# Later tiles' decayed keys and normed output: turned by VectorE blocks and a pass through DRAM in place of TensorE

## The chip, the cores and the metric

One core of a Trainium2 chip runs the whole program. The metric is the device time of one execution in microseconds (us); lower is better. The engines are named as in the profile: PE is TensorE (PEld its weight load), DVE is VectorE, ACT is ScalarE, POOL is GpSimd, SP is SyncE, which here issues nearly all DMAs.

## The reference, cut to what matters

Three stages follow each other. The first is gated linear attention over 4 sequences of 768 tokens with 8 heads of 48; the second a gated feed-forward layer on the normed output; the third a mixture of 8 experts, one per token.

```python
for t in range(S):
    state = alpha[:, :, t, :, None] * state + np.einsum('bhd,bhe->bhde', k[:, :, t], v[:, :, t])
    y[:, :, t] = np.einsum('bhd,bhde->bhe', q[:, :, t], state)
...
xn = x / rms * rms_g
g = xn @ w_gate
silu = g * (1.0 / (1.0 + np.exp(-g)))
val = xn @ w_val
return (silu * val @ w_out).astype(np.float32)
...
h = np.maximum(x[mask] @ w1[e], 0.0)
ye = h @ w2[e]
out[mask] = gate_w[mask, None] * eom[mask, e, None] * ye
```

## The kernel before, in words

The 3072 tokens are 24 tiles of 128 (t = 0 to 23). Tiles 0 to 17 go round over three sequences, so tile t is chunk t // 3 of sequence t % 3; tiles 18 to 23 are the fourth sequence in order. Chunk 5 of a sequence (tiles 15, 16, 17 and 23) is final and leaves no state behind.

**Attention of a tile.** Ahead of it comes the prework (`prework`, L365): alpha, k and q arrive by DMA, in `blk_a`, `blk_k`, `blk_q` from tile 7 on (`PET`, L239 to L260, twelve DMAs a tile), DVE turns them by 32x32 blocks (L386) so that the head dimension lies on partitions and tokens along the row, two scans on DVE (L315, L325) form the decays `Z` and `aT`, and two products (L407) the decayed keys `kT` and queries `qT`. Then `stages` (L411) has five stages:

- `score`: 8 matmuls `ps_s` (L426); DVE masks them into `P0`, `P1` (L436).
- `ktr`: 4 transposes on PE of `kT` into `ps_k` (L446), which ACT copies to `kn` (L448). Final tiles have none.
- `outp`: matmuls `ps_y` (L460, L464); ACT and POOL make the normed rows `xn` (L470 to L473).
- `state`: 8 matmuls `ps_st` (L485) from `kn` and `v`, added to the state by DVE (L492).
- `xtr`: 3 transposes on PE of `xn` into `ps_x` (L506). ACT scales them by `gT` (L512) and writes the high half `xh` (L513), DVE the low half `xl` (L514).

From tile 6 on `outp` and `state` share a place (`four`, L848).

**Feed-forward.** Three tiles are one group of 384 columns, whose `xh` and `xl` it needs. A group has 12 units; each is nine matmuls `ps_g`, nine `ps_v` (both at L608) and nine `ps_o` of the unit before (L642). ACT makes `tt` from `ps_g` (L600), DVE multiplies it with `ps_v` (L619), ACT writes `hh` (L622), DVE `hl` (L628). `ps_g` and `ps_v` have one PSUM bank each, so `tt` of a unit must be done with `ps_v` when the next unit's `ps_v` starts, and `hh` and `hl` when the next unit's `ps_o` starts.

**Order.** From the third group on (loop at L1091) one stage of attention is due every 2.4 slots, a slot being the nine matmuls of one kind, and `LEADG` says by how many slots the stages run ahead. PE keeps the order in which the matmuls were written (`seq`); on DVE, ACT and SP a scheduler orders the instructions when the program is built, and each engine then runs its list in order, as SP does with the DMAs: one that waits holds up those behind it. The eight experts follow from some 560 us on.

Of the kernel before, what the change touches and what calls it, by code (L numbers as in the profile page):

```python
# [40 lines left out]
    'TS': 3,  # L41
    'RA': 7,
    'RB': 9,
    'LEADG': 6,
    'NAT': 5,
    'XO': 2,
    'MT': 6,
    'STRICT': 4,
    'PET': 7,
    'NO': 'arkq',  # L50
}


# [2 lines left out]
def gla_glu_moe_kernel(  # L56
# [118 lines left out]
    def f(x):  # L175
        return x.bitcast(F32)
# [27 lines left out]

    vt = {}
    pre = {}
    xT = {}
    SEATS = CFG['SEATS']
    spread = [True]
    strict = [False]  # L210
# [93 lines left out]
    def flat(x):  # L304
        return x.rearrange("p a b -> p (a b)")
# [59 lines left out]
    def prework(t):  # L365
        if t < NAT:
            w = prework_nat(t)
            for x in CFG['NO']:
                yield w[x]
            return  # L370
        aT = att.tile([P, NP, P], F32, tag="aT", name="aT", bufs=CFG["ZBUF"])
        Z = att.tile([P, NP, P], F32, tag="A", name="Z", bufs=CFG["ABUF"])
        qT = att.tile([P, NP, P], F32, tag="qT", name="qT", bufs=2)
        kT = att.tile([P, NP, P], F32, tag="kT", name="kT", bufs=2)

        def tr(dst, nm):
            if t < PET:
                ps = bank([P, NP, P], "ps_n")
                src = rowt[nm].rearrange("p (a h) d -> p a (h d)", h=2)
                for p in range(NP):  # L380
                    nc.tensor.transpose(ps[:, p, :], src[:, p, :], ident)
                ins = nc.scalar.activation(dst, ps, AF.Copy)
                if t + 1 < PET:
                    load_tile(t + 1, nm)
                return ins
            return nc.vector.transpose(out=dst.rearrange("a p (c j) -> a p j c", j=TW),  # L386
                                in_=blk[nm].rearrange("a p (j d) -> a p j d", d=D)[:, :, :, 0:32])
        def tr_qk():
            tr(kT, "k")
            tr(qT, "q")  # L390
            if PET <= t + 1 < NTILE:
                load_tile(t + 1)
        def tra():
            now[0] = t
            ins = tr(aT, 'a')
            if t >= PET:
                pace(f'sc{t}', ins)
        yield tra
        yield tr_qk
        def sc():  # L400
            now[0] = t
            nc.gpsimd.memset(Z[:, NP - 1, P - 1:P], 1.0)
            pre[t] = (after_scan(Z, aT), qT, kT)
        yield sc
        yield lambda: upto_scan(aT, Z, aT)
        def mul(o, i):
            pace('km%d' % t, nc.vector.tensor_tensor(out=o, in0=o, in1=i, op=ALU.mult))  # L407
        yield lambda: mul(kT, Z)
        yield lambda: mul(qT, aT)

    def stages(t):  # L411
        b, c = place_of[t]
        first, final = c == 0, c == NCH - 1
        en, qT, kT = pre[t]
        Sc = state_of[b % BS]
        S_ = wide[0]
        rs = [slice(64 * hh, 64 * hh + D) for hh in range(2)]
        g, ti = divmod(t, GT)
        Pt = {}

        def score():
            ps = [bank([P, NP, P], "ps_s") for _ in range(2)]
            for p in range(NP):
                for hh in range(2):
                    r = slice(64 * hh, 64 * hh + D)
                    seq(nc.tensor.matmul(ps[hh][:, p, :], lhsT=kT[r, p, :], rhs=qT[r, p, :], start=True, stop=True))  # L426

            def post():
                if not first:
                    nc.vector.tensor_tensor(out=Sc, in0=Sc, in1=en.to_broadcast([P, NP, D]), op=ALU.mult)  # L430
                    for hh in range(2):
                        nc.scalar.activation(S_[rs[hh], :, hh * D:hh * D + D], Sc[rs[hh]], AF.Copy)
                mb = mask.to_broadcast([P, NP, P])
                for hh in range(2):
                    Ph = seat_of(t, f"P{hh}", [P, NP, P])
                    pace(f'Ph{t}', nc.vector.tensor_tensor(out=Ph, in0=ps[hh], in1=mb, op=ALU.mult))  # L436
                    Pt[hh] = Ph
            return post
        yield score

        def ktr():
            if final:
                return None
            ps = bank([P, NP, P], "ps_k")
            for p in range(NP):
                seq(nc.tensor.transpose(ps[:, p, :], kT[:, p, :], ident))  # L446
            kn = seat_of(t, "kn", [P, H, 64])
            nc.scalar.activation(kn, ps.rearrange("p a (h d) -> p (a h) d", h=2), AF.Copy)  # L448
            Pt["kn"] = kn
            return None  # L450
        yield ktr

        halves = (slice(0, 64), slice(64, P))

        def outp():
            ps = bank([P, DM], "ps_y")
            if not first:
                for p in range(NP):
                    for u in halves:
                        seq(nc.tensor.matmul(ps[u, p * 2 * D:p * 2 * D + 2 * D], lhsT=qT[:, p, u], rhs=S_[:, p, :],  # L460
                                         start=(p == 0), stop=False, skip_group_check=True))
            for h in (0, 2, 4, 6, 1, 3, 5, 7):
                for u in halves:
                    seq(nc.tensor.matmul(ps[u, h * D:h * D + D], lhsT=Pt[h % 2][:, h // 2, u], rhs=vt[t][:, h, :],  # L464
                                     start=first, stop=True, skip_group_check=True))

            def post():
                xn = seat_of(t, "xn", [P, DM])
                ss = att.tile([P, 1], F32, tag="ss", name="ss", bufs=2)
                pace(f'xs{t}', nc.scalar.activation(xn, ps, AF.Square, accum_out=ss))  # L470
                nc.gpsimd.tensor_scalar(out=ss, in0=ss, scalar1=1.0 / DM, scalar2=1e-6, op0=ALU.mult, op1=ALU.add)  # L471
                pace(f'ss{t}', nc.gpsimd.tensor_tensor(out=ss, in0=ss, in1=mhalf, op=ALU.pow))
                pace(f'xa{t}', nc.scalar.activation(xn, ps, AF.Copy, scale=ss[:, 0:1]))  # L473
                Pt["xn"] = xn
            return post
        yield outp

        def state():
            if final:
                return None  # L480
            kn = Pt["kn"]
            ps = bank([P, NP, D], "ps_st")
            for p in range(NP):
                for hh in range(2):
                    seq(nc.tensor.matmul(ps[64 * hh:64 * hh + 64, p, :], lhsT=kn[:, 2 * p + hh, :],  # L485
                                     rhs=vt[t][:, 2 * p + hh, :], start=True, stop=True))

            def post():
                if first:
                    nc.scalar.activation(Sc, ps, AF.Copy)  # L490
                else:
                    nc.vector.tensor_tensor(out=Sc, in0=ps, in1=Sc, op=ALU.add)  # L492
            return post
        yield state

        def xtr():
            if t and t + 2 < NTILE:
                load_v(t + 2)
            if ti == 0:
                xT[g] = (act.tile([P, KD, G], F32R, tag="xh", name="xh"),  # L500
                         act.tile([P, KD, G], F32R, tag="xl", name="xl"))
            xh, xl = xT[g]
            xn = Pt["xn"]
            ps = bank([P, KD, P], "ps_x")
            for kc in range(KD):
                seq(nc.tensor.transpose(ps[:, kc, :], xn[:, kc * P:kc * P + P], ident))  # L506
            sl = slice(ti * P, ti * P + P)

            def post():
                xf = xn.rearrange("p (a b) -> p a b", a=KD)  # L510
                for kc in range(KD):
                    pace(f'xg{t}', nc.scalar.activation(xf[:, kc, :], ps[:, kc, :], AF.Copy, scale=gT[:, kc:kc + 1]))  # L512
                pace(f'xh{t}', nc.scalar.activation(xh[:, :, sl], xf, AF.Copy))  # L513
                pace(f'xl{t}', nc.vector.tensor_tensor(out=xl[:, :, sl], in0=xf, in1=f(xh[:, :, sl]), op=ALU.subtract))  # L514
            return post
        yield xtr


    late = []

# [341 lines left out]
            return None  # L862
        return s_, k_, yd_, no_, x_

    att_stream = (st for t in range(GT, NTILE) for st in (four if t >= CFG['MT'] else stages)(t))
    nprep = GT + 1
    AHEAD = CFG['AHEAD']
    done = 0
# [222 lines left out]
    for g in range(2, NG):  # L1091
# [15 lines left out]
        for n in range(3 * KF):  # L1107
            post = slot(g + 2, n)
            if post:
                post()  # L1110
            if done < (NTILE - GT) * NST and ((g - 1) * 3 * KF + n + 1 + CFG['LEADG']) * GT >= (done + 1 - GT * NST) * 3 * KF / NST:
                post = stage()
                if post:
                    post()
# [274 lines left out]
```

## Time and profile before

| | |
|---|---|
| median of 3 runs | 851.7 us (851.08 to 854.45) |
| profiled execution, its own time | 854.62 us |
| its span, first to last instruction | 852.8 us |
| PE busy | 836.4 us (98%) |
| DVE busy | 493.9 us (58%) |
| ACT busy | 324.0 us (38%) |
| mean granted TensorE clock | 0.993 of full speed |

"Busy" is the time in which an engine runs at least one instruction. PE's matmuls overlap, so their cost is read from the distances of their starts, not from their durations. A releaser in square brackets names what ended an engine's idle time.

### The profile page before, as it was taken

The numbers are of one execution on the slowest core, as the hardware profiler recorded it, in microseconds if no ns is written. First come the engines' busy times: TensorE is split into PE (matmuls) and PEld (weight loads), VectorE is DVE, ScalarE is ACT, GpSimd is POOL, SyncE is SP. The second block draws the span as 40 slices with busy tenths as digits, with TensorE's granted clock in tenths as the row PEclk, the third lists the DMA queues.
The fourth block names the chain that finished last, engine by engine and source line by source line (L and its number), as shares of the span: only waits on it lengthen the run. The fifth ranks groups of instructions, "written<-read, shape, count | busy, mean of one in ns | idle before, by whom it ended". The sixth has DMA issues, their size and how long they took to land.

```text
span 852.8 us, 15908 instructions
## 1 busy us (share of the span) xinstructions
PE 836.4 (98%) x6196; PEld 802.5 (94%) x6196; DVE 493.9 (58%) x1111; ACT 324.0 (38%) x705; POOL 147.4 (17%) x204
## 2 busy tenths in 40 slices
PE   7999999999999999999999999999999999999996
PEld 6899999999999999999999999999998999999996
DVE  6899989496855656765666552243444342443341
ACT  1655544334233333332432332333235342454441
POOL 2001001001200100010010010013033242343351
PEclk8999999999999999999999999999999999999999
DMA  9955573872411322232232000042055164266421
GB/s 193 181 155 155 166 176 85 224 180 71 114 45 41 82 57 65 49 84 62 61 89 61 10 29 1 2 124 71 8 198 191 56 218 132 75 204 203 148 69 36
DMA packets 120269, 88.97 MB, mean 104 GB/s; under 512 B 55291, under 2 KB 115324, under 8 KB 120192
## 3 DMA queue, kind: packets, MB, share of 16 engines
q1 hardware_dynamic: 115728, 78.46, 35.2%
q0 software_dynamic: 4464, 9.48, 3.2%
q8 instruction: 49, 0.80, 0.4%
q14 instruction: 28, 0.23, 0.1%
HBM read 72.11 MB, written 16.07 MB: 103 GB/s over the span
## 4 chain that ended last, share of the span: by engine, by line
PE 80%; DMA 6%; DVE 5%; issue 4%; ACT 2%; POOL 1%; SPq 1%; POOLq 0%; DVEq 0%; ACTq 0%
PE ps_o L642 18%; PE ps_v L608 17%; PE ps_g L608 17%; PE ps_b L1071 8%; PE ps_h L608 7%; PE ps_s L426 3%; DMA st<-in_moe_w_dram 3%; PE ps_y L464 3%; PE ps_y L460 2%; DMA out_dram<-ob,ix 1%; DMA er<-bucket 1%; PE ps_x L506 1%; PE ps_k L446 1%; PE ps_st L485 1%; DMA blk_q<-in_q_dram 1%
## 5 line engine op out<-in xcount | busy, mean ns | idle before, releaser
L619 DVE TENSOR_TENSOR tt<-tt,ps_v 128x384 f32<-128x384 f32 x96 | 52.9, 551 | 123.2 <-PE ps_v L608 111.9
L622 ACT ACTIVATE hh<-tt 128x384 fp32r<-128x384 f32 x96 | 50.3, 524 | 132.0 <-DVE tt L619 124.7
L600 ACT ACTIVATE tt<-ps_g 128x384 f32<-128x384 f32 x96 | 47.1, 490 | 121.3 <-PE ps_g L608 116.2
L628 DVE TENSOR_TENSOR hl<-tt,hh 128x384 fp32r<-128x384 f32 x96 | 54.4, 566 | 27.4 <-ACT hh L622 26.7
L1056 DVE SCALAR_TENSOR_TENSOR h<-ps_h,h 128x256 fp32r<-128x256 f32 (+6 forms) x72 | 38.0, 531 | 54.2 <-ACT h L1055 53.8
L608 PE MATMUL ps_g<-xh,wgh 128*128 128x384 f32 x192 | 67.9, 354 | 0.0
L608 PE MATMUL ps_v<-xh,wvh 128*128 128x384 f32 x192 | 65.7, 342 | 1.4 <-DVE tt L619 1.4
L1071 PE MATMUL ps_b<-w2a,h 128*128 128x384 f32 (+2 forms) x336 | 66.6, 339 | 0.5 <-ACT h L1055 0.5
L642 PE MATMUL ps_o<-woh,hh 128*128 128x400 f32 x192 | 66.6, 355 | 0.0
L642 PE MATMUL ps_o<-wol,hh 128*128 128x400 f32 x192 | 66.4, 346 | 0.0
L1071 PE MATMUL ps_b<-w2b,h 128*114 128x384 f32 (+3 forms) x336 | 65.2, 338 | 0.4 <-ACT h L1055 0.2
L608 PE MATMUL ps_g<-xh,wgl 128*128 128x384 f32 x192 | 65.0, 338 | 0.1
L608 PE MATMUL ps_v<-xh,wvl 128*128 128x384 f32 x192 | 64.9, 338 | 0.0
L608 PE MATMUL ps_g<-xl,wgh 128*128 128x384 f32 x192 | 64.8, 338 | 0.0
L608 PE MATMUL ps_v<-xl,wvh 128*128 128x384 f32 x192 | 64.7, 337 | 0.0
L642 PE MATMUL ps_o<-woh,hl 128*128 128x400 f32 x192 | 63.4, 344 | 0.0
L1071 PEld LDWEIGHTS ps_b<-w2b,h 128*114 128x114 f32 (+3 forms) x336 | 57.4, 175 | 2.6 <-ACT h L1055 0.6
L1071 PEld LDWEIGHTS ps_b<-w2a,h 128*128 128x128 f32 (+2 forms) x336 | 57.7, 181 | 1.6 <-ACT h L1055 1.0
L608 PE MATMUL ps_h<-x,w1b 128*128 128x456 f32 (+3 forms) x288 | 58.6, 344 | 0.1
L1055 ACT ACTIVATE h<-ps_h 128x256 fp32r<-128x256 f32 (+6 forms) x72 | 33.3, 467 | 62.1 <-PE ps_h L608 57.3
L471 POOL TENSOR_SCALAR ss<-ss 128x1 f32<-128x1 f32 x24 | 8.2, 341 | 273.6 <-ACT xn L470 268.7
L608 PE MATMUL ps_h<-x,w1a 128*128 128x256 f32 (+3 forms) x288 | 53.6, 328 | 0.0
(284 smaller groups left out, 1966.6 us busy)
## 6 DMA issues: line engine op xcount, KB each, us to landing
st<-in_moe_w_dram SPq DMA_DIRECT2D x64, 384.0 KB
bucket<-zero SPq DMA_DIRECT2D x8, 772.0 KB
stg<-in_moe_w_gate_dram SPq DMA_DIRECT2D x12, 384.0 KB
stg<-in_moe_w_val_dram SPq DMA_DIRECT2D x12, 384.0 KB
stg<-in_moe_w_out_dram SPq DMA_DIRECT2D x12, 384.0 KB
v<-in_v_dram SPq DMA_DIRECT2D x23, 192.0 KB
blk_a<-in_alpha_dram SPq DMA_DIRECT2D x34, 96.0 KB
blk_k<-in_k_dram SPq DMA_DIRECT2D x34, 96.0 KB
```

Of the source, the lines that this page charges most:

```text
L426: seq(nc.tensor.matmul(ps[hh][:, p, :], lhsT=kT[r, p, :], rhs=qT[r, p, :], start=True, stop=True))
L460: seq(nc.tensor.matmul(ps[u, p * 2 * D:p * 2 * D + 2 * D], lhsT=qT[:, p, u], rhs=S_[:, p, :], start=(p == 0), stop=False, skip_group_check ...
L464: seq(nc.tensor.matmul(ps[u, h * D:h * D + D], lhsT=Pt[h % 2][:, h // 2, u], rhs=vt[t][:, h, :], start=first, stop=True, skip_group_check= ...
L600: nc.scalar.activation(tt, ps, AF.Silu)
L608: seq(nc.tensor.matmul(ps, lhsT=a_[:, kc, :], rhs=b_[:, kc, :], start=(n == 0), stop=(n == 3 * KD - 1)))
L619: nc.vector.tensor_tensor(out=tt, in0=tt, in1=ps, op=ALU.mult)
L622: nc.scalar.activation(hh, tt, AF.Copy)
L628: nc.vector.tensor_tensor(out=hl, in0=tt, in1=f(hh), op=ALU.subtract)
L642: seq(nc.tensor.matmul(obank[s][i], lhsT=a_[:, sl], rhs=weight(b_, j), start=(j == j0 and n == 0), stop=(j == j1 - 1 and n == 2)))
L1055: nc.scalar.activation(hh[:, 0, :], ps, AF.Relu)
L1056: nc.vector.scalar_tensor_tensor(out=hh[:, 1, :], in0=ps, scalar=0.0, in1=f(hh[:, 0, :]), op0=ALU.max, op1=ALU.subtract)
L1071: ins = nc.tensor.matmul(ob2[u][i][0:r], lhsT=hh[:, a_, sl], rhs=we[p][b_][:, j, :], start=(j == 0 and m == 0), stop=(j == KF2 - 1 and m = ...
```

## The change

From tile 9 on (`DT`) no tile is turned by PE, but for tile 9's keys.

- Keys: `turn_k(t + 1)` in the fourth stage of tile t. DVE turns `kT` by 32x32 blocks into `Z`, which is free by then; four DMAs write it to a DRAM buffer in runs of 32 floats (128 bytes, 512 runs each), so placed that the blocks come to lie where the full transpose wants them; one DMA reads the buffer back as `kn`. Tiles 10 to 14 and 18 to 22: ten times.
- Rows: `turn_x` in the fifth stage. DVE turns `xn` into the space of `P0`, four DMAs of 384 runs of 128 bytes write it to DRAM, one reads it back into `xn`. `put_x`, in the second stage of the next tile, does the scaling, `xh` and `xl`, from SBUF. Tiles 9 to 23: fifteen times.
- `LEADG` goes from 6 to 11 slots, and two stages are added at the end for the last tile's `put_x`.
- Tile 7's turns of `blk_k` and `blk_q`, the first from the block buffers, keep the order of the source on DVE.

```diff
-    'LEADG': 6,
+    'LEADG': 11,
+    'DT': 9,
...
-            return nc.vector.transpose(out=dst.rearrange("a p (c j) -> a p j c", j=TW),
+            ins = nc.vector.transpose(out=dst.rearrange("a p (c j) -> a p j c", j=TW),
                                 in_=blk[nm].rearrange("a p (j d) -> a p j d", d=D)[:, :, :, 0:32])
+            if t == PET and nm != "a":
+                tc.keep_in_program_order(ins)
+            return ins
...
-            kn = Pt["kn"]
+            kn = Pt["kn"] if "kn" in Pt else kq.pop(t)
...
+        def turn_x():
+            if t + 2 < NTILE:
+                load_v(t + 2)
+            xn, xb = Pt["xn"], flat(Pt[0])[:, 0:DM]
+            nc.vector.transpose(out=xb.rearrange("p (a k i) -> p k a i", a=TW, k=KD),
+                                in_=xn.rearrange("p (k d a) -> p k a d", a=TW, k=KD))
+            mid = dram.tile([P, KD * P], F32, tag="mid_x", name="mid_x", bufs=2)
+            dst = mid.rearrange("(d a) (k c i) -> c d (a k) i", a=TW, k=KD, c=TW)
+            for c in range(TW):
+                nc.sync.dma_start(dst[c], xb[32 * c:32 * c + 32].rearrange("d (n i) -> d n i", i=32))
+            nc.sync.dma_start(xn, mid)
+
+        def put_x():
+            group()
+            xh, xl = xT[g]
+            xf = Pt["xn"].rearrange("p (a b) -> p a b", a=KD)
+            sl = slice(ti * P, ti * P + P)
+            for kc in range(KD):
+                nc.scalar.activation(xf[:, kc, :], xf[:, kc, :], AF.Copy, scale=gT[:, kc:kc + 1])
+            nc.scalar.activation(xh[:, :, sl], xf, AF.Copy)
+            nc.vector.tensor_tensor(out=xl[:, :, sl], in0=xf, in1=f(xh[:, :, sl]), op=ALU.subtract)
+        moves[t] = (turn_x, put_x)
...
+    def turn_k(t):
+        Z, kT = spare[t], pre[t][2]
+        nc.vector.transpose(out=flat(Z).rearrange("a (c p d) -> a p c d", c=TW, p=NP),
+                            in_=kT.rearrange("a p (j c) -> a p c j", c=TW))
+        mid = dram.tile([P, H * 64], F32, tag="mid_k", name="mid_k", bufs=2)
+        dst = mid.rearrange("(j c) (p a d) -> a j (c p) d", c=TW, p=NP, a=TW)
+        for a in range(TW):
+            nc.sync.dma_start(dst[a], flat(Z)[32 * a:32 * a + 32].rearrange("j (n d) -> j n d", d=32))
+        kn = att.tile([P, H, 64], F32, tag="kn", name="kn")
+        nc.sync.dma_start(flat(kn), mid)
+        kq[t] = kn
...
+    def moved(t):
+        s_, k_, y_, d_, _ = stages(t)
+        def second():
+            if t == DT:
+                k_()
+            return laid.pop() if laid else None
...
+        def keys_():
+            while prep:
+                prep_step()
+            if t + 1 < NTILE and place_of[t + 1][1] < NCH - 1:
+                turn_k(t + 1)
+        def rows_():
+            moves[t][0]()
+            laid.append(moves[t][1])
+        return s_, second, yd_, keys_, rows_
```

How the built order moves is shown at three places. In the changed kernel the lines have other numbers: L386 is L389, L315 is L318, L325 is L328, L619 is L666, L622 is L669, L628 is L675, L600 is L647; the block turns of keys and rows are L556 and L512, their writes L561 and L517, their reads L563 and L518, the scaling of the read rows L526.

DVE at tile 7, in the second group, before; `F` and `Fo` are weights being unpacked:

```order
L534 SCALAR_TENSOR_TENSOR Fo<-stg,Fo 128x384
L386 STREAM_TRANSPOSE qT<-blk_q 128x4x4x32
L386 STREAM_TRANSPOSE kT<-blk_k 128x4x4x32
L531 SCALAR_TENSOR_TENSOR F<-stg,F 128x384
L619 TENSOR_TENSOR tt<-tt,ps_v 128x384
```

And now, from the same `Fo` on, and then from the row where the turns stand:

```order
L581 SCALAR_TENSOR_TENSOR Fo<-stg,Fo 128x384
L578 SCALAR_TENSOR_TENSOR F<-stg,F 128x384
L666 TENSOR_TENSOR tt<-tt,ps_v 128x384
L581 SCALAR_TENSOR_TENSOR F<-stg,F 128x384
L675 TENSOR_TENSOR hl<-tt,hh 128x384
```

```order
L666 TENSOR_TENSOR tt<-tt,ps_v 128x384
L389 STREAM_TRANSPOSE aT<-blk_a 128x4x4x32
L389 STREAM_TRANSPOSE kT<-blk_k 128x4x4x32
L389 STREAM_TRANSPOSE qT<-blk_q 128x4x4x32
L581 SCALAR_TENSOR_TENSOR F<-stg,F 128x384
L578 SCALAR_TENSOR_TENSOR Fo<-stg,Fo 128x384
```

The two turns stood ahead of the product `tt` of a unit; they now stand behind the `tt` of the second unit after it.

DVE at tile 20, before (`state` is the running state, `en` and `begin` small helpers of the scans):

```order
L386 STREAM_TRANSPOSE qT_5676<-blk_q_1470 128x4x4x32
L628 TENSOR_TENSOR hl_5537<-tt_5522,hh_5536 128x384
L492 TENSOR_TENSOR state0_122<-ps_st_5564,state0_122 128x192
L407 TENSOR_TENSOR qT_5426<-qT_5426,aT_5424 128x512
L430 TENSOR_TENSOR state0_122<-state0_122,en_5494 128x192
L386 STREAM_TRANSPOSE aT_5674<-blk_a_1467 128x4x4x32
L312 COPY en_5744<-aT_5674 128x4
L313 MEMSET aT_5674 128x4
L315 SCALAR_TENSOR_TENSOR Z_5675<-aT_5674,begin_127 128x511
L318 TENSOR_TENSOR en_5744<-en_5744,Z_5675 128x4
L324 RECIPROCAL begin_127<-Z_5675 128x4
L325 SCALAR_TENSOR_TENSOR aT_5674<-aT_5674,begin_127 128x512
```

And now:

```order
L675 TENSOR_TENSOR hl_5505<-tt_5489,hh_5504 128x384
L556 STREAM_TRANSPOSE Z_5408<-kT_5410 128x4x4x32
L389 STREAM_TRANSPOSE qT_5663<-blk_q_1470 128x4x4x32
L499 TENSOR_TENSOR state0_122<-ps_st_5543,state0_122 128x192
L414 TENSOR_TENSOR qT_5409<-qT_5409,aT_5407 128x512
L437 TENSOR_TENSOR state0_122<-state0_122,en_5473 128x192
L389 STREAM_TRANSPOSE aT_5661<-blk_a_1467 128x4x4x32
L512 STREAM_TRANSPOSE P0_5424<-xn_5552 128x3x4x32
L315 COPY en_5727<-aT_5661 128x4
L316 MEMSET aT_5661 128x4
L318 SCALAR_TENSOR_TENSOR Z_5662<-aT_5661,begin_127 128x511
L666 TENSOR_TENSOR tt_5570<-tt_5570,ps_v_5572 128x384
```

Two block turns have come in, and the first scan (L318) now writes a `Z` out of which the four writes of the keys are still reading, ahead of the unit's `tt`. SP's list for the same tile, now:

```order
L561 DMA mid_k<-Z 512x1x32 x4
L365 DMA v<-in_v_dram 128x8x48
L263 DMA blk_q<-in_q_dram 32x4x192
L263 DMA blk_q<-in_q_dram 32x4x160
L563 DMA kn<-mid_k 128x512
L263 DMA blk_a<-in_alpha_dram 32x4x192
L517 DMA mid_x<-P_5424 384x1x32 x4
L263 DMA blk_a<-in_alpha_dram 32x4x160
L263 DMA blk_a<-in_alpha_dram 32x4x192
L518 DMA xn<-mid_x 128x384
```

The ten DMAs of the two turns stand among the loads of the next tile's blocks, and each read back waits on SP for its four writes.

ACT at tile 20, before, from the normed rows (L473) on:

```order
L473 ACTIVATE xn<-ps_y,ss 128x384
L432 ACTIVATE wide_125<-state_122 48x4x48 x2
L600 ACTIVATE tt<-ps_g 128x384
L622 ACTIVATE hh<-tt 128x384
L512 ACTIVATE xn<-ps_x,gT 128x128 x3
L513 ACTIVATE xh<-xn 128x3x128
L600 ACTIVATE tt<-ps_g 128x384
```

And now (`xn` scaled at L526 from what the DMA brought back):

```order
L480 ACTIVATE xn<-ps_y,ss 128x384
L439 ACTIVATE wide_125<-state_122 48x4x48 x2
L647 ACTIVATE tt<-ps_g 128x384
L669 ACTIVATE hh<-tt 128x384
L647 ACTIVATE tt<-ps_g 128x384
L526 ACTIVATE xn<-xn,gT 128x128 x3
L527 ACTIVATE xh<-xn 128x3x128
L669 ACTIVATE hh<-tt 128x384
L647 ACTIVATE tt<-ps_g 128x384
```

The scaling stood one unit behind the normed rows and waited for PE; it now stands behind the second unit's `tt`, mostly ahead of its `hh`, and waits for a DMA.

## Rows read from the trace of the kernel before

**Rows 1.** The page's first part: busy time, share and instructions of each engine.
```profile
PE 836.4 (98%) x6196; PEld 802.5 (94%) x6196; DVE 493.9 (58%) x1111; ACT 324.0 (38%) x705; POOL 147.4 (17%) x204
```
**Rows 2.** Busy time by stretch: PE, PEld, DVE, ACT, POOL, clock, DMA share, GB/s.
```profile
115.00:170.00 55.00, 53.55 (x430) 51.09 (x429) 41.84 (x85) 22.14 (x54) 3.01 (x10) 1.00 0.57 153
230.00:260.00 30.00, 30.00 (x234) 29.19 (x233) 19.12 (x37) 10.21 (x25) 1.59 (x5) 1.00 0.30 71
400.00:490.00 90.00, 90.00 (x749) 86.81 (x748) 55.02 (x125) 30.83 (x74) 7.45 (x14) 1.00 0.21 52
```
**Rows 3.** Timeline of PE around one tile's key transposes: start, duration, instruction.
```profile
407.09 0.34 PE L608 MATMUL ps_v<-xh,wvle 128*128 128x384 f32 x1
...
407.89 0.34 PE L642 MATMUL ps_o<-wole,hh 128*128 128x400 f32 x1
```
**Rows 4.** Timeline of PE at tile 19, from the unit ahead of its output on.
```profile
435.49 0.34 PE L608 MATMUL ps_v<-xh,wvl 128*128 128x384 f32 x1
...
438.24 0.34 PE L642 MATMUL ps_o<-wol,hh 128*128 128x400 f32 x1
...
439.70 0.33 PE L608 MATMUL ps_g<-xh,wgh 128*128 128x384 f32 x1
...
444.28 0.34 PE L642 MATMUL ps_o<-woh,hl 128*128 128x400 f32 x1
444.46 0.49 PE L506 MATMUL ps_x<-ident,xn 128*128 128x128 f32 x3
...
444.97 0.34 PE L608 MATMUL ps_g<-xl,wgh 128*128 128x384 f32 x1
```
**Rows 5.** Timelines of DVE and of PE at tile 7.
```profile
116.41 1.11 DVE L386 STREAM_TRANSPOSE qT<-blk_q 128x512 f32<-128x512 f32 x1 [2.74 <-DMA blk_q<-in_q_dram]
...
119.33 0.44 PE L608 MATMUL ps_v<-xh,wvh 128*128 128x384 f32 x1 [1.45 <-DVE tt L619]
```
**Rows 6.** Groups on DVE, 230 to 545 us: busy, mean ns, idle before.
```profile
L325 DVE TENSOR_TENSOR_SCAN aT<-aT,begin 128x512 f32<-128x512 f32 x12 | 14.6, 1220 | 0.2
...
L386 DVE STREAM_TRANSPOSE kT<-blk_k 128x512 f32<-128x512 f32 x11 | 12.1, 1099 | 0.0
...
L407 DVE TENSOR_TENSOR kT<-kT,Z 128x512 f32<-128x512 f32 x12 | 8.0, 668 | 0.0
```
**Rows 7.** Timelines of DVE and ACT at tile 19.
```profile
435.93 0.56 DVE L619 TENSOR_TENSOR tt<-tt,ps_v 128x384 f32<-128x384 f32 x1 [3.24 <-PE ps_v L608]
436.69 1.14 DVE L386 STREAM_TRANSPOSE qT<-blk_q 128x512 f32<-128x512 f32 x1 [0.20 <-PE ps_y L460]
...
439.54 0.58 ACT L473 ACTIVATE xn<-ps_y,ss 128x384 f32<-128x384 f32 x1 [1.36 <-POOL ss L472]
...
445.05 0.88 ACT L512 ACTIVATE xn<-ps_x,gT 128x128 f32<-128x128 f32 x3
```
**Rows 8.** SP's issues, and DMA busy tenths in 40 slices of 405 to 415 us.
```profile
406.46 1.74 SPq L260 DMA_DIRECT2D blk_q<-in_q_dram  x4
...
DMA  0000000001687578730037776697100000000020
```
**Rows 9.** DMA queue of SP over the run, and over 0 to 8 us: packets, MB, share.
```profile
q1 hardware_dynamic: 115728, 78.46, 35.2%
...
q1 hardware_dynamic: 5668, 1.07, 102.2%
```
**Rows 10.** A load of 386 KB issued by SP, and the DVE instruction that waited for it.
```profile
622.40 0.36 SPq L1017 DMA_DIRECT2D er<-bucket  x1
...
625.68 0.17 DVE L1025 CAST ix<-er 128x2 int32<-128x2 f32 x1 [3.88 <-DMA er<-bucket]
```
**Rows 11.** Timeline of PE around one tile's scores.
```profile
402.67 0.34 PE L642 MATMUL ps_o<-wohe,hl 128*128 128x400 f32 x1
402.94 1.16 PE L426 MATMUL ps_s<-qT,kT 48*128 48x128 f32 x16
...
404.32 0.34 PE L608 MATMUL ps_g<-xl,wghe 128*128 128x384 f32 x1
```

More of the change, by code (lines that the diff above doesn't have):

```diff
@@ L206, in gla_glu_moe_kernel @@
     pre = {}
+    spare = {}
     xT = {}
+    moves = {}
     SEATS = CFG['SEATS']
@@ L403, in sc @@
             pre[t] = (after_scan(Z, aT), qT, kT)
+            spare[t] = Z
         yield sc
@@ L494, in stages, with group @@
         yield state
+        def group():
+            if ti == 0:
+                xT[g] = (act.tile([P, KD, G], F32R, tag="xh", name="xh"),
+                         act.tile([P, KD, G], F32R, tag="xl", name="xl"))
+        def turn_x():
[19 more added lines that the diff above has]
+        moves[t] = (turn_x, put_x)
         def xtr():
@@ L498, in xtr @@
                 load_v(t + 2)
-            if ti == 0:
-                xT[g] = (act.tile([P, KD, G], F32R, tag="xh", name="xh"),
-                         act.tile([P, KD, G], F32R, tag="xl", name="xl"))
+            group()
             xh, xl = xT[g]
@@ L516, in stages @@
         yield xtr
+    kq = {}
+    def turn_k(t):
[9 more added lines that the diff above has]
+        kq[t] = kn
     late = []
@@ L863, in four, with yd_, post, rest @@
         return s_, k_, yd_, no_, x_
-    att_stream = (st for t in range(GT, NTILE) for st in (four if t >= CFG['MT'] else stages)(t))
+    DT = CFG['DT']
+    laid = []
+    def moved(t):
[4 more added lines that the diff above has]
+            return laid.pop() if laid else None
+        def yd_():
+            posts = [y_(), d_()]
+            def post():
+                for p in posts:
+                    if p:
+                        p()
+            return post
+        def keys_():
[7 more added lines that the diff above has]
+        return s_, second, yd_, keys_, rows_
+    def rest():
+        yield lambda: None
+        yield lambda: laid.pop()
+    att_stream = (st for t in range(GT, NTILE + 1)
+                  for st in (rest() if t == NTILE else moved(t) if t >= DT else
+                             four(t) if t >= CFG['MT'] else stages(t)))
     nprep = GT + 1
@@ L1110, in gla_glu_moe_kernel @@
                 post()
-            if done < (NTILE - GT) * NST and ((g - 1) * 3 * KF + n + 1 + CFG['LEADG']) * GT >= (done + 1 - GT * NST) * 3 * KF / NST:
+            if done < (NTILE - GT) * NST + 2 and ((g - 1) * 3 * KF + n + 1 + CFG['LEADG']) * GT >= (done + 1 - GT * NST) * 3 * KF / NST:
                 post = stage()
```

## The prediction
> **What bounds the kernel now.** The page's first part comes first: PE is busy for 98% of the span, DVE for 58%, ACT for 38% [rows 1]. The busy times by stretch say where PE has room: from 400 to 490 us it is busy for 90.00 of 90.00 us at a clock of 1.00, while DVE has 35 us of the same stretch free and DMA four fifths; from 115 to 170 us, with DVE at 51.09 of 55 us, PE still lacks only 1.45 us [rows 2]. So in the stage that changes nothing waits; the time is the number of PE's instructions, and what leaves PE comes off the end one for one, provided that no new wait takes its place. The rest of the reading is therefore about waits: the timelines of PE, DVE and ACT around one tile, and SP's issues with the DMA's load beside them.
>
> **What PE sheds.** The four transposes of keys lie between the `ps_v` at 407.09 and the `ps_o` at 407.89 [rows 3]. Without them the distance would be that of two neighbours, 0.17 + 0.18 us, so they cost 0.80 - 0.35 = 0.45, of which I take 0.44 for rounding. The three of rows lie between 444.28 and 444.97 [rows 4]: 0.69 - 0.36 = 0.33. Ten tiles by 0.44 and fifteen by 0.33 are 4.4 + 4.9 = **9.3 us**.
>
> **Tile 7.** DVE stands 2.74 us in the turn of `blk_q`, waiting for its DMA, with `tt` behind it; PE then lacks 1.45 us, released by that `tt` [rows 5]. Put behind the second `tt` after it, the turn finds its data landed. At most 1.45 us come back, none if the weight conversions that fill DVE there (93% busy) are late next. I take the middle, **0.7**.
>
> **What is added.** DVE gets a turn of 512 columns (1.10 us, as its turns of `blk_k` [rows 6]) ten times and one of 384, by the same rate 0.82, fifteen times: 11.0 + 12.3 = 23 us over more than 300 us in which it is some 40% free. ACT loses ten copies and scales from SBUF instead of PSUM; nothing waits for it. Both cost nothing as work; what counts is where they stand. The last scan's `Z` becomes the buffer of the turned keys, so the next scan must wait for their writes; `xh` waits for two DMAs in series. At tile 9 the larger lead puts five stages close together: 3.9 us of DVE (its work of two further stages) into the 30 us from 230, of which 10.9 are free [rows 2]; I set that at nothing (0 to 4). If that cover is gone, `tt` is late.
>
> **The keys' chain.** Time runs from the end of a tile's state matmuls. In the new order they follow a unit's `ps_o`. Output and state take 2.40 us of PE (438.24 - 0.18 less 435.49 + 0.17 [rows 4]) and a slot of `ps_o` nine times 0.18, 1.62, so that unit's `ps_v` ends at -4.02; its `tt` starts 0.27 later, as at 435.93 [rows 7], at -3.75. DVE has `tt` 0.56, a product of 0.67, `hl` 0.55 and then the turn of 1.10, which ends at about -0.9. SP issues at 0.43 us a DMA (four in 1.74) and data flow 0.85 us after the first issue [rows 8]: from about 0.05 on. The four writes are 2048 packets of 128 bytes, 128 for each of 16 DMA engines. No write of that size is in the trace. The nearest row is the first 8 us, when loads of 192 bytes a packet keep the queue at 102.2% for 5668 packets: 1.022 x 8 x 16 / 5668 = 23 ns each [rows 9]. So 2.9 us. An ending: a load of 386 KB releases DVE 3.28 us after its issue [rows 10]; less 0.85 and 1.5 for its bytes (78.46 MB in 35.2% of 16 x 852.8 us, 16.3 bytes a ns), 0.9 us is left. The writes have landed at 0.05 + 2.95 + 0.9 = **3.9**.
>
> The scan waits for this at the head of DVE, with the end's copy, the reciprocal, and `tt` behind it. PE reaches the `ps_v` that needs its bank at 6.33 (a `ps_g` and a `ps_v`, together 3.14, which is 439.70 to 444.28 less eight `ps_o` of 0.18 [rows 4]; a `ps_o` of 1.62 and a `ps_g` of 1.57), by which `tt` must be done. `tt` 0.55, small ones 0.17 + 0.17 and the scan 1.22 [rows 6] leave **4.4** as the latest start. Half a microsecond to spare: the keys cost nothing at 23 ns a packet and begin to cost at 27; each further ns costs 0.128 us in each of ten tiles.
>
> **The rows' chain.** The normed rows are ready 0.58 us after 439.54 [rows 7], at 2.06; DVE's turn is behind a product of 0.67 and a turn of 1.14 and ends at 3.5. SP stands meanwhile in the read of `kn`, which waits until 3.9 for its writes, then issues a load, and the first row write at 4.8. Data from 5.6, 96 packets an engine, 2.2 us, ending 0.9: 8.7. The read back takes 0.85 + 0.75 + 0.9: **11.2**. Who waits is ACT's scaling, queued ahead of `hh` or just behind it. PE wants `hh` at the `ps_o` of that unit, which starts after two units (3.14 + 1.62 each), a `ps_g` and a `ps_v` of 1.57 and the next tile's scores, 404.32 - 402.94 - 0.08 = 1.30 us [rows 11]: at 13.96. The scaling was 0.88 us [rows 7] and `hh` must follow, so 11.9 to 12.4 is the latest start; 0.7 to 1.2 us to spare. So they cost nothing either. SP's loads of the next tile's blocks stand behind the two reads and go out some 5 to 9 us later than now; a tile lasts five stages of 2.4 slots, some 19 us, and their turns come in the next.
>
> **The sum.** The profiled execution took 854.62 us, its span 852.8, and is 2.9 above the median of the runs. From it go 9.3 + 0.7 = 10.0, leaving 844.6; from the median of 851.7, **841.7 us**.
>
> **Where the price is uncertain.** 23 ns is for reads from DRAM at 192 bytes. Below it nothing is gained, since PE sets the pace. The upper end is the queue's mean over the whole run, 35.2% of 852.8 x 16 us for 115728 packets [rows 9], 41.5 ns, though those packets average 678 bytes. By it the keys land at 6.3, 1.9 us too late, and the rows, behind them on SP, at 15.3, which is 1.1 to 1.6 too late even after PE's 1.9: some 3.2 us a tile for ten tiles and 1 for the rest, so 841.7 + 33 = 875. What is gained is used up at 33 ns. I take 23 because its row has small packets with the queue full, as here; the 41.5 is mostly of larger ones. The DMA's load beside the writes is another tile's blocks: the tenths stay at 7 or 8 for a few slices only [rows 8].
>
> The Trainium skill, page "DMA: Bandwidth & Descriptors", section "Specifications", says that transfers under 512 bytes do not reach line rate because the DMA engine reads, modifies and writes; that speaks against turning by runs of 128 bytes. By that rule a packet would carry a read and a write; if that doubled 23 to 46 ns, an estimate, the sum would be near 880 in place of 841.7. The trace has only loads at this size, so it neither bears this out nor contradicts it.
>
> **Rivals.**
>
> - *Dear writes.* At over 33 ns a packet the next scan and with it `tt` waits for the keys' DMA, then PE at `ps_v`; DVE's room doesn't help since it stands in line. 34 ns gives about 857, 38 ns 866, 41.5 ns 875; I work with 38: **866, slower**. For: short writes to DRAM are not in the trace, and margins are half a microsecond. Against: 23 ns at a full queue. The sentence on the skill's page above is this rival's rule. Chance 0.22.
> - *Small stalls.* The order puts turns and DMAs a little later than I worked out, and 0.3 to 1 us of PE goes in 10 to 15 tiles: 846 to 853, say **849**. For: no margin is above 1.2 us. Chance 0.16.
> - *DVE crowded at tile 9*: 2 to 5 us lost once, 844 to 848, **846**. Against: 10.9 us free. Chance 0.06.
> - *The change brings PE nothing.* PE's freed time is filled by waiting for DVE in each group as now by transposes: **851**. Against: 90.00 busy of 90.00 without any wait, and DVE at 61% [rows 2]. Chance 0.03.
>
> **How the numbers follow.** The forecast, no steady wait, has 0.53; its own range is 839 (all of tile 7, a little of DVE's and ACT's smoothing) to 847. Two of ten may be left out, so the range goes from 838.5 over small stalls and the cheaper part of the dear writes up to 864, below 38 ns. A measurement can tell 0.5%, 4.3 us, from no change: faster is below 847.4, slower above 856. Faster: 0.53, the crowding's most and a few of the small stalls, 0.61. Slower: the dear writes, 0.22. Same: the rest of the small stalls and the last rival, 0.17.
>
> **What would show it.** Right: no `ps_x` after tile 8's and no `ps_k` after tile 9's; PE at 100% in the same stretches; `tt` there released by `ps_v`; the first scan without idle time before it, or with such that ends over 1.6 us before `ps_v` is due; the ACT scaling released by its DMA ahead of need; four writes of keys over in about 4 us; PE's idle at tile 7 gone or under 0.8. Wrong: idle time of PE "<- DVE `tt`" once a tile with the scan "<- DMA `mid_k`" ahead of it (dear writes, some 1 us or more each); PE idle "<- ACT `hh`" with the scaling "<- DMA `xn`" ahead of it (rows too late); SP's reads of `kn` later than 4 us after the first write; PE idle only between the second and third group (crowding).

## The result, and the profile after

The changed kernel takes **864.92 us** (median of 4 runs, 863.17 to 868.31) against 853.08 (851.08 to 854.8) for the kernel before in the same comparison: a ratio of 1.0144, 95% interval 1.01 to 1.0189. It is slower, where 841.7 was forecast, and lies just above the range of 838.5 to 864. The profiled execution has a span of 864.5 us.

The page's first part, and the busy times by stretch (PE, PEld, DVE, ACT, POOL, clock, DMA share, GB/s), which answer to [rows 1] and [rows 2]:

```profile
PE 835.1 (97%) x6111; PEld 794.0 (92%) x6111; DVE 513.5 (59%) x1136; ACT 315.9 (37%) x695; POOL 147.3 (17%) x204
```

```profile
115.00:170.00 55.00, 55.00 (x439) 52.87 (x439) 42.16 (x87) 24.00 (x56) 2.14 (x10) 1.00 0.60 163
230.00:260.00 30.00, 26.50 (x210) 24.98 (x209) 16.45 (x30) 7.76 (x19) 1.35 (x3) 0.94 0.43 95
400.00:490.00 90.00, 87.22 (x713) 82.09 (x712) 59.67 (x126) 28.22 (x71) 7.53 (x14) 1.00 0.41 93
```

PE has the 85 instructions less. At tile 7 it no longer stops (55.00 of 55). But where it was busy without a gap it now lacks 3.50 of 30 us in the third group and 2.78 of 90 later. Who is waited for stands in the view of PE's waits (us in total, times, longest):

```profile
PE ps_o L689 <- ACT hh L669: 6.0, 5, 3.5
PE ps_v L655 <- DVE tt L666: 4.6, 5, 1.5
...
PE ps_v L655 <- DVE ohc L739: 1.6, 1, 1.6
```

The third row is one more stop at `ps_v` behind a late DVE. With it PE stops eleven times for over 0.2 us between the second group and the experts, 12.1 us of idle time in all; the kernel before has no such stop there.

And in the same view of ACT and of DVE:

```profile
ACT xn L526 <- DMA xn<-mid_x: 74.2, 15, 8.5
```

```profile
DVE hl L675 <- ACT hh L669: 42.5, 36, 6.3
DVE xl L528 <- ACT xh L527: 36.5, 9, 5.9
DVE Z L318 <- DMA mid_k<-Z: 8.8, 7, 2.4
```

The same view of the kernel before:

```profile
DVE hl L628 <- ACT hh L622: 26.7, 46, 0.9
...
DVE xl L514 <- ACT xh L513: 13.6, 14, 1.7
```

All fifteen scalings of rows find ACT waiting for their DMA, 74.2 us together, and DVE behind it waits 42.5 us in `hl` and 36.5 in `xl`, where it waited 26.7 and 13.6 before. Two places on the timelines of ACT and of PE, tile 10 (the largest stop) and tile 19 (a stop of middling size, though its rows' writes are the slowest of the fifteen):

```profile
225.65 0.47 ACT L647 ACTIVATE tt<-ps_g 128x384 f32<-128x384 f32 x1
234.65 0.98 ACT L526 ACTIVATE xn<-xn,gT 128x128 f32<-128x128 f32 x3 [8.53 <-DMA xn<-mid_x]
235.67 0.52 ACT L527 ACTIVATE xh<-xn 128x384 fp32r<-128x384 f32 x1
236.09 0.51 ACT L669 ACTIVATE hh<-tt 128x384 fp32r<-128x384 f32 x1
...
452.49 0.99 ACT L526 ACTIVATE xn<-xn,gT 128x128 f32<-128x128 f32 x3 [5.99 <-DMA xn<-mid_x]
...
453.94 0.51 ACT L669 ACTIVATE hh<-tt 128x384 fp32r<-128x384 f32 x1
```

```profile
232.81 0.34 PE L655 MATMUL ps_v<-xh,wvl 128*128 128x384 f32 x1
236.65 0.70 PE L689 MATMUL ps_o<-woh,hh 128*128 128x400 f32 x1 [3.50 <-ACT hh L669]
...
454.50 0.45 PE L689 MATMUL ps_o<-woh,hh 128*128 128x400 f32 x1 [0.90 <-ACT hh L669]
```

At tile 10 ACT stands in the scaling for 8.53 us; the `hh` of a unit is behind it in the list, and PE's `ps_o` waits for that `hh`. At tile 19 the same with 5.99 and 0.90 us. SP's issues at tile 19:

```profile
438.23 2.58 SPq L561 DMA_DIRECT2D mid_k<-Z  x4
440.91 0.56 SPq L365 DMA_DIRECT2D v<-in_v_dram  x1
441.57 1.04 SPq L263 DMA_DIRECT2D blk_q<-in_q_dram  x2
442.79 0.34 SPq L563 DMA_DIRECT2D kn<-mid_k  x1
...
443.65 2.54 SPq L517 DMA_DIRECT2D mid_x<-P  x4
...
449.77 0.34 SPq L518 DMA_DIRECT2D xn<-mid_x  x1
```

Four writes take SP 2.5 to 2.6 us here, not the 1.74 of four block loads [rows 8]; from the first row write to the read back, which waits for all four, 6.1 us go by, and to the scaling 8.8. Over the fifteen tiles the time from first write to read back is 4.1 to 6.1 us, with a median of 4.8.

**A ruler.** All kernels have the same 96 units on PE, so the time between the same two `ps_g` of the profiled execution is a measure free of start and end. From the first `ps_g` of the 19th unit to that of the 85th (163.61 to 548.04 before, 162.21 to 557.68 after) lie tiles 9 to 23; from the 6th to the 19th lies tile 7. Before: 384.43 and 84.82 us. After: 395.48 and 83.11. So tile 7 gave 1.7 us and the later tiles cost 11.05, where 9.3 were to be gained: some 20 us were lost there.

### The profile page after: what moved, and what is told of

Its sections match the earlier page's. It is cut to its first block, busy times and chain, and to the rows that moved or that the text cites. A ratio compares the mean times of both kernels' runs of the same rounds, so it can differ in the third digit from the quotient of the medians.

```text
span 864.5 us, 15986 instructions
## 1 busy us (share of the span) xinstructions
PE 835.1 (97%) x6111; PEld 794.0 (92%) x6111; DVE 513.5 (59%) x1136; ACT 315.9 (37%) x695; POOL 147.3 (17%) x204
## 4 chain that ended last, share of the span: by engine, by line
PE 57%; DMA 14%; DVE 12%; issue 6%; SPq 5%; ACT 4%; POOL 2%; POOLq 0%; DVEq 0%; ACTq 0%
PE ps_o L689 12%; PE ps_v L655 11%; PE ps_g L655 10%; PE ps_b L1155 9%; PE ps_h L655 8%; DMA xn<-mid_x 3%; DMA mid_x<-P 3%; DMA st<-in_moe_w_dram 3%; SPq L517 2%; SPq L561 2%; PE ps_s L433 2%; PE ps_y L471 2%; DMA er<-bucket 1%; DMA out_dram<-ob,ix 1%; ACT xn L526 1%
## 5 line engine op out<-in xcount | busy, mean ns | idle before, releaser
L669 ACT ACTIVATE hh<-tt 128x384 fp32r<-128x384 f32 x96 | 50.1, 522 | 142.4 <-DVE tt L666 139.7
L666 DVE TENSOR_TENSOR tt<-tt,ps_v 128x384 f32<-128x384 f32 x96 | 52.4, 545 | 71.3 <-PE ps_v L655 62.0
L675 DVE TENSOR_TENSOR hl<-tt,hh 128x384 fp32r<-128x384 f32 x96 | 54.3, 566 | 43.4 <-ACT hh L669 42.5
L647 ACT ACTIVATE tt<-ps_g 128x384 f32<-128x384 f32 x96 | 46.6, 486 | 46.4 <-PE ps_g L655 40.3
```

The costliest lines, as they stand in the source:

```text
L647: nc.scalar.activation(tt, ps, AF.Silu)
L666: nc.vector.tensor_tensor(out=tt, in0=tt, in1=ps, op=ALU.mult)
L669: nc.scalar.activation(hh, tt, AF.Copy)
L675: nc.vector.tensor_tensor(out=hl, in0=tt, in1=f(hh), op=ALU.subtract)
```

## The experiments

Theory A: ACT stands in the scaling of rows that are late, and what is behind it is late with them. Theory B: the scan's wait for the keys' writes (the first rival of the prediction). Theory C: DVE has too much to do. All medians are beside 853.1 (the changed kernel), 851.9, 853.3 or 853.5 us of the kernel before in the same comparison. "The jump" is the place near 205 us where the larger lead takes effect and the stages of several tiles come close together.

| kernel | us | ratio (95%) | 19th to 85th unit |
|---|---|---|---|
| before | | | 384.43 |
| changed | 864.92 | 1.0144 (1.01 to 1.0189) | 395.48 |
| scaling kept in source order | 845.13 | 0.9925 (0.9897 to 0.9952) | 376.76 |
| keys only | 845.51 | 0.9923 (0.9896 to 0.995) | 380.60 |
| rows only | 852.89 | 1.0002 (0.9982 to 1.0021) | 386.59 |
| long runs | 848.58 | 0.9948 (0.9922 to 0.9973) | 379.98 |
| `xl` kept | 862.63 | 1.0109 (1.0075 to 1.0143) | 394.52 |
| `v` later | 865.37 | 1.0144 (1.0111 to 1.0177) | 396.72 |
| kept, rows written twice | 852.75 | 1.0003 (0.998 to 1.0026) | 383.83 |
| no turns, lead 11 | 854.23 | 1.0004 (0.9979 to 1.003) | 388.13 |
| kept, keys in `P1` | 846.82 | 0.9919 (0.9892 to 0.9946) | 377.64 |
| kept, lead 8 | 851.57 | 0.9974 (0.9949 to 0.9999) | 380.54 |
| kept, lead 6 | 851.55 | 0.9967 (0.9941 to 0.9992) | 384.48 |

**The scaling kept in source order.**

```diff
-                nc.scalar.activation(xf[:, kc, :], xf[:, kc, :], AF.Copy, scale=gT[:, kc:kc + 1])
-            nc.scalar.activation(xh[:, :, sl], xf, AF.Copy)
+                tc.keep_in_program_order(nc.scalar.activation(xf[:, kc, :], xf[:, kc, :], AF.Copy, scale=gT[:, kc:kc + 1]))
+            tc.keep_in_program_order(nc.scalar.activation(xh[:, :, sl], xf, AF.Copy))
```

> ACT's scaling of the read rows and xh keep the order of the source, which puts them one unit later, behind that unit's hh; nothing else moves but xl on DVE. Theory A (ACT stands in the scaling until the rows' DMA is back, 74 us in all, and hh, hl and then tt behind it come late): most of the 20 us that PE loses between the second group's end and the experts go, 846 to 852 us, and hh no longer waits for ACT. Theory B (the scan's wait for the keys' writes, 8.8 us, makes tt late): 862 to 866, idle before the scan as in the changed kernel. Theory C (DVE is short of time for 23 us of turns): 861 to 866.

845.13 us. The stretch falls by 18.7 us against the changed kernel, with the same turns and the same lists on PE and SP, instruction by instruction. Tile 19 again, SP and ACT:

```profile
424.83 2.55 SPq L517 DMA_DIRECT2D mid_x<-P  x4
...
431.18 0.34 SPq L518 DMA_DIRECT2D xn<-mid_x  x1
```

```profile
435.78 0.52 ACT L669 ACTIVATE hh<-tt 128x384 fp32r<-128x384 f32 x1 [3.25 <-DVE tt L666]
436.21 0.97 ACT L526 ACTIVATE xn<-xn,gT 128x128 f32<-128x128 f32 x3
```

The rows' chain is as slow as before (6.35 us from first write to read), but the scaling is one unit further down, behind that unit's `hh` and the next one's, and starts without idle time. Only at tile 9 does ACT still stand long in it, 4.9 us, with no stop of PE behind. And DVE's waits are back where the kernel before had them:

```profile
DVE hl L675 <- ACT hh L669: 25.0, 44, 0.6
...
DVE xl L528 <- ACT xh L527: 13.7, 14, 1.8
```

Theory A holds; B and C fall as the cause of the 20 us. B's mechanism is there all the same, once, with 0.64 us for PE:

```profile
379.88 1.22 DVE L318 TENSOR_TENSOR_SCAN Z<-aT,begin 128x511 f32<-128x511 f32 x1 [2.31 <-DMA mid_k<-Z]
381.02 0.53 DVE L666 TENSOR_TENSOR tt<-tt,ps_v 128x384 f32<-128x384 f32 x1
```

```profile
381.60 0.45 PE L655 MATMUL ps_v<-xh,wvhe 128*128 128x384 f32 x1 [0.64 <-DVE tt L666]
```

**Keys only**: the fifth stage is `xtr` again.

```diff
-        return s_, second, yd_, keys_, rows_
+        return s_, second, yd_, keys_, x_
```

> Keys turned through DRAM, rows by PE as before, lead 11 and tile 7's order as in the change. Theory A: the gain of the keys alone, 4.4, and of tile 7, 1.7: 845 to 849 us, no stall of PE of over 0.5 us from 250 to 545 us. Theory B: the scan's wait stays, 855 to 866. Theory C: between, 850 to 856.

845.51 us. Of DVE's waits:

```profile
DVE Z L318 <- DMA mid_k<-Z: 14.7, 8, 3.0
```

The scan waits even longer for the keys' writes than in the changed kernel, and PE idles for 0.09 us in the whole compared stretch: DVE's slack covers it. B falls a second time.

**Rows only**: `second` runs `k_()` for every tile and `turn_k` is not called.

```diff
-            if t == DT:
-                k_()
-            return laid.pop() if laid else None
+            posts = [k_()] + ([laid.pop()] if laid else [])
...
-                turn_k(t + 1)
```

> Rows turned through DRAM, keys by PE as before. Theory A: stalls at hh stay, smaller by what the keys' writes and read took ahead of the rows on SP and in the queue (some 2 us earlier): 852 to 863 us. Theory B: without the keys' writes no stall, 845 to 849. Theory C: 850 to 856.

852.89 us, with ACT still waiting:

```profile
ACT xn L526 <- DMA xn<-mid_x: 60.4, 15, 6.5
```

The rows are scaled a median of 7.2 us after their turn on DVE ends (8.7 in the changed kernel; fifteen tiles, ends of L512 to starts of L526 in the timelines). Without keys on SP ahead of them they come 1.6 us earlier (first write to read: median 4.2 instead of 4.8), and most of the loss goes, not all: against 384.43 less the 4.9 of the rows, some 7 us are still lost, part of them behind two stops at the jump (0.67 and 0.58 us).

**Long runs.**

```diff
-        dst = mid.rearrange("(j c) (p a d) -> a j (c p) d", c=TW, p=NP, a=TW)
+        dst = mid.rearrange("(a j) (n d) -> a j n d", a=TW, d=32)
...
-            dst = mid.rearrange("(d a) (k c i) -> c d (a k) i", a=TW, k=KD, c=TW)
+            dst = mid.rearrange("(c d) (n i) -> c d n i", c=TW, i=32)
```

> The writes of both turns go to DRAM in rows of 1536 or 2048 bytes instead of runs of 128; same bytes, same number of DMAs, so keys and rows come back only turned within their blocks of 32: the turn across the blocks is left out. If the short runs are what makes the rows late (issues of 0.63 us in place of 0.43, 43520 packets): rows back 2 us earlier or more, 848 to 855 us. If it is two passes in series behind the loads of v and of the next blocks: rows back under 1 us earlier, 859 to 864.

This kernel leaves out the turn across the blocks; bytes, DMAs and their order are those of the change. 848.58 us: with the scaling where it was, 15.5 of the 18.7 us come back. First write to read takes a median of 3.5 us instead of 4.8, turn to scaling 7.7. The short runs cost each set of four writes 1.3 us, about what was missing. Some 0.8 of it lies in SP's four issues, 0.42 us each instead of 0.62. The rows came 1 to 1.3 us earlier, less than the 2 that I had put beside this range of times.

**`xl` kept**: of `put_x` only the low half on DVE keeps the order of the source.

```diff
-            nc.vector.tensor_tensor(out=xl[:, :, sl], in0=xf, in1=f(xh[:, :, sl]), op=ALU.subtract)
+            tc.keep_in_program_order(nc.vector.tensor_tensor(out=xl[:, :, sl], in0=xf, in1=f(xh[:, :, sl]), op=ALU.subtract))
```

> Of the changed kernel only the low half xl on DVE keeps the order of the source, which puts it one unit later; ACT's scaling and every other engine's order stay as in the change. If the late rows cost in two ways, by hh on ACT and by xl at the head of DVE with masks, turn and tt behind it: the stalls of PE at ps_v (some 7 us with their after-effects) go, those at ps_o (some 11) stay, 855 to 860 us. If only ACT's queue matters: 863 to 866. If only DVE's: 846 to 850.

862.63 us, and stops at `ps_v` as before:

```profile
PE ps_v L655 <- DVE tt L666: 6.3, 6, 1.6
```

My account of two separate paths falls. DVE only waits one instruction later:

```profile
DVE hl L675 <- ACT hh L669: 80.5, 45, 6.5
```

`hl` needs the `hh` that stands behind the scaling on ACT. The one place on ACT feeds both kinds of stop.

**`v` later**: `load_v(t + 2)` moved from `turn_x` into `put_x`.

```diff
         def turn_x():
-            if t + 2 < NTILE:
-                load_v(t + 2)
...
         def put_x():
+            if t + 2 < NTILE:
+                load_v(t + 2)
```

> The changed kernel with the load of v (192-byte packets) issued behind the rows' read back instead of ahead of their writes. If the queue of other loads ahead of the row writes makes them late: rows back 0.5 to 1.5 us earlier and a third of the 19 us lost comes back, 857 to 862 us. If only the chain's own issues and passes count: 863 to 866.

865.37 us; first write to read 4.5 instead of 4.8 us, and turn to scaling no shorter (8.9 us). The load of `v` by itself is not what the rows wait for.

**Kept, rows written twice.**

```diff
-            for c in range(TW):
+            for c in [*range(TW)] * 2:
```

> The kernel with the kept scaling, each write of rows issued twice: eight DMAs a tile, the rows back some 3 us later. The kept order had 1.5 to 5 us between the rows' return and their scaling. If only the place of the waiting instruction matters: 844 to 849 us, no steady stall. If the writes cost by themselves (the DMA queues, SP, SBUF): 853 or more.

852.75 us: just short of the 853 for writes that cost by themselves, and by a mechanism that I had not named. First write to read took 8.0 us; the scaling was mostly covered, but a second place showed itself:

```profile
DVE P L443 <- DMA mid_x<-P: 14.7, 6, 4.8
```

The writes read out of `P0`, and a later mask into `P0` now waits for them, with `tt` behind it. The same shape again, on DVE.

**No turns, lead 11**: the kernel before with the two edits that have no DMA in them.

```diff
-    'LEADG': 6,
+    'LEADG': 11,
...
+            if t == PET and nm != "a":
+                tc.keep_in_program_order(ins)
```

> The kernel before with tile 7's turns in source order and a lead of 11 slots, without any pass through DRAM. The idle time at tile 7 goes and nothing takes its place: 1.5 to 1.7 us faster in the second group; the lead alone moves stages and costs nothing or under 0.5 us: 849.5 to 851.5 us.

854.23 us, where 849.5 to 851.5 was expected. Tile 7 gave its 1.7 us (83.14 for 84.82), but the lead cost 3.7, all of it at the jump:

```profile
212.03 1.50 PE L429 MATMUL ps_s<-qT,kT 48*128 48x128 f32 x16 [2.09 <-DVE kT L410]
```

DVE is busy without a gap for 4 us ahead of this and its products come late: the prediction's rival of a crowded DVE, in this kernel. Behind the stop PE ran at a granted clock of 0.50 for a while, which costs nearly as much as the stop (see the last section).

**Kept, keys in `P1`**: `turn_k` writes into the tile's second mask buffer.

```diff
-        Z, kT = spare[t], pre[t][2]
+        Z, kT = half[t - 1][1], pre[t][2]
```

> The kernel with the kept scaling, keys turned into the space of the tile's P1 instead of Z, so that the next scan no longer waits for their writes (6.9 us of DVE's time there, with one stall of PE of 0.8 us behind it). If that wait is the rest of the loss: no idle time before the scan, 0.5 to 1.0 us less between the second group and the experts, 843 to 846 us. If the masks now wait for the writes instead: 846 to 850.

846.82 us, 377.64 for the stretch instead of 376.76. The scan no longer waits, and nothing is gained: two stops of 0.7 and 0.8 us, at the jump (195 and 217 us), stand in place of the one of 0.64.

**Kept, lead 8 and lead 6**: only the number changed.

> The kernel with the kept scaling, the stages 8 slots ahead instead of 11. The lead alone seemed to cost 1.2 us beside a stall; the rows, scaled 3 slots (4.7 us) ahead of their group, are still in time: 844 to 846 us, the same or 1 us less than with 11. If the rows come too late for their group: PE idle at the group's first ps_g, 847 to 852.

> The same with the lead of 6 of the kernel before: scaling and xh one slot (1.6 us) ahead of the group take 1.5 and xl 0.6, so PE waits some 0.5 to 1 us at each of five groups: 846 to 851 us. If the scheduler's order leaves them in time: 844 to 846.

851.57 and 851.55 us. With 6, PE waits at the start of four groups:

```profile
404.57 0.44 PE L655 MATMUL ps_g<-xh,wgh 128*128 128x384 f32 x1 [1.07 <-ACT xh L527]
```

So the pass through DRAM needs a longer lead than 6. With 8 that stop is gone, so its median lies where rows too late were expected, but not for that reason; one of 2.3 us at 217 us has come:

```profile
PE ps_v L655 <- DVE tt L666: 2.7, 2, 2.3
```

By median and by the stretch 11 was the best of the three. The version with the scaling kept in order beats both kernels: by the ruler it gains 7.7 us in the later tiles and 1.7 at tile 7, so 9.4 of the 10.0 that were forecast; its median is 6.8 lower.

## Why the prediction was wrong, by its own steps

- **What PE sheds**, 4.4 and 4.9: right. Unit by unit, keys only is 0.44 to 0.45 us shorter than the kernel without turns at nine of ten tiles; the tenth lies in that kernel's stop at the jump. The kept kernel is 0.33 shorter than keys only at twelve of fifteen tiles; at the other three something else is mixed in, among it the stop of 0.64 us.
- **Tile 7**, 0.7 (0 to 1.45): under-sized. It gave 1.7 us. The stop itself was 1.45; nothing was late next, and what follows a stop is saved too: its unit became 1.65 us shorter.
- **What is added costs nothing as work**: right. The kept kernel has all the turns and passes, and PE is busy 90.00 of 90.00 us from 400 to 490.
- **The keys' chain**, landed at 3.9: right, partly by luck. At tile 19 the last of the state's matmuls starts at 438.94 and the read of `kn` leaves SP at 442.79, 3.85 later, by two errors that cancel: issues of 0.63 us instead of 0.43, and packets at 13.3 ns instead of 23. (The trace times each packet; this is the mean of the 43520 of 128 bytes.) The rival of dear writes, at 38 ns, gave nearly the measured time (866) by a mechanism that did not happen. Two of the sums do not come out of their own terms: 6.33 less 0.55, 0.17, 0.17 and 1.22 is 4.2, not 4.4, and 3.2 for ten tiles and 1 for five is 37, not 33. Neither bears on the miss.
- **The rows' chain is the step that failed.** "The first row write at 4.8" was right (4.7 at tile 19); "Data from 5.6, 96 packets an engine, 2.2 us, ending 0.9: 8.7" came to 10.8 there, and the scaling to 13.5 instead of 11.2. First write to read was reckoned at 3.9 for every tile; it took 4.1 to 6.1, median 4.8. The term that was left out is the other traffic in the queue, which the prediction had put at "a few slices only". Busy times as above over that time, at tile 15 (the quickest) and at tile 19 (the slowest):

```profile
348.19:352.27 4.08, 4.08 (x25) 4.08 (x24) 1.69 (x4) 1.02 (x2) 0.00 (x0) 1.00 0.45 76
443.65:449.77 6.12, 6.12 (x37) 6.12 (x36) 3.38 (x9) 1.02 (x2) 3.02 (x3) 1.00 1.01 231
```

With a DMA share of 0.45 the chain took 4.08 us, near the 3.9 (slower issues and cheaper packets cancel here too); with 1.01 it took 6.12. In rows only, without the keys' transfers, the median is 4.2. That is not the whole of it: tile 22 took 5.5 with a share of 0.48, tile 20 4.1 with 0.80, and why stays open. The Trainium skill, page "DMA: Bandwidth & Descriptors", section "Specifications", says that short transfers fall short of line rate. The trace agrees: 128 bytes in 13.3 ns are 9.6 bytes a ns, where the queue's mean was reckoned at 16.3. The doubling to 46 ns that the prediction estimated from that section does not show.
- **The margin was read as if its miss cost its own size.** "11.9 to 12.4 is the latest start; 0.7 to 1.2 us to spare" was about right: at tile 19 a start at 13.5 made PE idle for 0.90. But it had to hold in fifteen tiles whose chains differ by 2 us, and a stop costs more than its idle time. At tile 19 the first `ps_o` started 1.24 us after the last `ps_v` instead of 0.18, and the next three distances were 0.29, 0.36 and 0.28 instead of 0.18: the unit was 1.45 us longer. At tile 10 PE idles 3.50 us and then takes 3.14 for nine `ps_o` (236.65 to 239.79) instead of 1.62; and `hl` and `tt` on DVE slip with `hh`, which is the second kind of stop. Together 18.7 us, of which 12.1 are idle time.
- Of the rivals, "small stalls" is the nearest in mechanism: it had the order's waits a little late, with 0.3 to 1 us in 10 to 15 tiles. It was under-sized, at 849 us.
- The signs to look for were the right ones: "PE idle `<- ACT hh` with the scaling `<- DMA xn` ahead of it (rows too late)" is what the trace shows. The scaling's place in ACT's list was known before the run. That the scheduler put it there because it expected the data by then is likely, but no run shows what it expected.

## What to carry to other kernels

Where an in-order engine waits for a DMA, look at what stands behind the waiting instruction, and move that instruction down before making the DMA faster: the same late rows cost 19 us ahead of a unit's `hh` and some 1.6 us one unit later, while the faster writes in the old place won back 15.5. A margin of a microsecond was none here, on a chain whose first pass alone varied by 2 us from tile to tile; take the slowest pass seen, not the reckoned one. Price a stop on TensorE with what comes after it.

## What had not been expected of the hardware

The granted clock after a stop, in the changed kernel at tile 10 (columns as above):

```profile
231.00:236.60 5.60, 2.15 (x17) 1.71 (x13) 0.54 (x3) 1.92 (x6) 0.00 (x0) 0.98 0.37 100
236.60:239.40 2.80, 2.75 (x8) 2.59 (x9) 2.80 (x6) 0.38 (x2) 0.00 (x0) 0.50 0.00 0
```

After 3.5 us of idling PE ran at 0.50, the lower of its two levels (1.2 GHz), over the whole second stretch: 1.5 us on top of the stop. The other stops of this kernel, of up to 1.6 us, had no such stretch behind them. In other kernels shorter stops did: 2.09 us without turns at lead 11, 2.17 with the rows written twice, 1.79 with `v` later. The stop of 2.31 us in the kept kernel at lead 8 did not. Behind the stop at lead 11 without turns, and behind the one in the kept kernel at lead 8:

```profile
212.70:216.10 3.40, 3.40 (x18) 3.18 (x15) 3.23 (x8) 0.00 (x0) 0.00 (x0) 0.50 0.28 74
```

```profile
217.00:222.00 5.00, 4.98 (x64) 4.72 (x66) 4.23 (x11) 2.04 (x5) 2.28 (x3) 1.00 0.16 53
```

So the length of a stop alone did not tell what it would cost.

The profiled executions also differ at their start. The first 20 us before and of the kept kernel, which have the same PE list there:

```profile
0.00:20.00 20.00, 15.03 (x100) 11.71 (x101) 14.08 (x35) 2.70 (x5) 5.68 (x45) 0.87 1.20 193
```

```profile
0.00:20.00 20.00, 15.16 (x124) 11.44 (x125) 14.86 (x37) 3.20 (x6) 6.24 (x45) 1.00 1.20 191
```

With the clock at 0.87 there the 6th unit starts at 78.79 us, at 1.00 at 75.65. These 3.1 us come ahead of all that the change touches and are no merit of a kernel, which is why stretches of PE's own list were compared above. What decides it was not tried.
